# Moving the load of w1 behind GpSimd's filter copies and its half of V's reorder

## The chip, the cores and the metric

The kernel runs on one core of one Trainium2 chip. The core has five engines that matter here: TensorE (PE, matmuls; PEld is its weight load), VectorE (DVE), ScalarE (ACT), GpSimd (POOL) and SyncE (SP), and 16 DMA engines that all queues share. The metric is the device time of one execution in microseconds (us), lower is better. Before the change it is 516.92 us, the median of 3 runs (514.62 to 517.74).

## The reference

Two blocks follow each other on x of 8 batches x 3136 rows x 256 columns. The first is a global filter: a Fourier transform along the 3136 rows, a product with a complex filter, and the inverse transform. The second mixes rows by a product of rank 32 (U, V) and then columns by two matrices with a ReLU between them:

```python
X = np.fft.rfft(x, axis=1)
Y = X * (filt_r + 1j * filt_i)[None]
x = np.fft.irfft(Y, n=3136, axis=1)            # output of the first block
h = x.transpose(0, 2, 1) @ U @ V               # rank 32
u = x + h.transpose(0, 2, 1)
out = u + np.maximum(u @ w_ch1, 0) @ w_ch2     # w_ch1 256x1024, w_ch2 1024x256
```

## The kernel before, in words

All arrays are float16, the output is float32. The transform of 3136 = 49 x 64 points is done in steps by matmul against constant matrices, one batch at a time:

- f1: over the 49, from the loaded x (tile `x`, four loads of 392 KB a batch, L128). For batches 0 and 1 its result is turned on TensorE (`turn`), for the others it goes through HBM.
- mid: over the 64 (pz, L384), the product with the filter (DVE `uv`, L392) and the inverse over the 64 (pe, L345). ScalarE copies the result into tiles `e` (L355), two frequencies k at a time. For each batch 12 such pairs are made; I call them pair 0 to pair 11. From `e`, SP writes them to HBM (`ct`, L364), two pairs in one DMA of 256 KB, and reads them back in another order into the tile `eb` (`load_e2`, L416), because the next step needs k along the partitions. Batch 0 differs: pairs 8, 9 and pair 10 are written by two DMAs (256 KB and 128 KB), and pair 11 goes straight from `e` into `eb` by four DMAs of 32 KB, two issued by GpSimd and two by SP (L359). The read back into `eb` of batch 0 comes in six DMAs: three for its first half (h=0) and three for its second (h=1).
- rank (ph, L423): the product with U, copied 64 times into `eb` by DVE (L438).
- s4 (pu, L456): the inverse over the 49 and the product with V together, 16 groups of 8 matmuls, from `eb` and the tile `sv`. `sv` holds the constants and V in another order of its columns; that reorder is done half by GpSimd and half by DVE (`v_rows`, L201). The first eight groups read the first half of `eb`, the other eight the second half.
- Then the two matrices, over 49 groups of 512 rows: mm1 (phh, L488) with `w1sb`, ReLU on ScalarE (L491), mm2 (pc, L544) with `w2sb`, and the residual (L536).

The schedule is written out by hand: each engine runs its instructions in the order in which the program emits them, and waits in front of one that isn't ready. Batch 0 runs alone as a prologue (lines 581 to 625); after that the plan (lines 564 to 659) deals the steps of the next batches between the matmuls of mm1 and mm2.

DMAs go through two queues. q0 holds what GpSimd issues: the loads of U, x, the filters (`fab`, three parts), V (`vnat`), the constants of `sv`, w1 and w2, and the stores of the output. q1 holds what SP issues: `ct` and `eb`. Within each queue, on each of the 16 DMA engines, the DMAs stand in order of issue. On SP, a read back into `eb` that waits for its `ct` writes also holds up the `ct` writes that the program emits behind it. SP's order in the prologue is: write pairs 0-1, 2-3, 4-5, 6-7; read back part 0 of h=0 (it waits for the writes of pairs 0-1 and 2-3); write pairs 8-9; write pair 10; read back part 1 of h=0; two rows of pair 11; read back part 2 of h=0 (it waits for the writes of pairs 8-9 and 10); then the three parts of h=1.

The second copy of the filter (partitions 64 to 127) is made by copies on the chip, `spread_filters` (L167): parts 0 and 1 by DVE and ScalarE, part 2 by GpSimd in four copies. Later on GpSimd wait the copies `seen` (L620): each reads a few elements of `eb`, and so holds GpSimd until a half of `eb` has landed; behind them come the other loads of x of batch 1 and the load of w2 (L623).

Of the kernel before, what the change touches and what calls it, by code (L numbers as in the profile page):

```python
# [80 lines left out]
def kernel(  # L81
# [11 lines left out]
    nc = tc.nc  # L93
# [31 lines left out]
    def load_x(b, c):  # L125
        t = sb.tile([98, 8 * DM], F16, tag="x", bufs=4, name="x")
        for a, n in ((0, 96), (96, 2)) if b == 0 else ((0, 98),):
            nc.gpsimd.dma_start(t[a:a + n], dram(x.tensor, (b * SEQ + 8 * c + 32 * a) * DM, [[32 * DM, n], [1, 8 * DM]]))  # L128
        xt[b, c] = t
# [30 lines left out]
    def spread_filters(i):  # L160
        s = slice(PARTS[i], PARTS[i + 1])
        copies = ((nc.vector.tensor_copy, nc.scalar.copy), (nc.vector.tensor_copy, nc.scalar.copy),
                  (nc.gpsimd.tensor_copy, nc.gpsimd.tensor_copy))[i]

        for s in (slice(PARTS[2], 19), slice(19, NK)) if i == 2 else (s,):
            for f, copy in enumerate(copies):
                copy(fab[64:128, f, s, :], fab[0:64, f, s, :])  # L167
# [12 lines left out]
    w1sb = cst.tile([128, 2, NH], F16)  # L180
# [19 lines left out]
    def v_rows(copy, a, z):  # L200
        copy(sv[0:RANK, a:z], vnat.rearrange("p (q r) -> p r q", r=NR)[:, a:z])  # L201
# [34 lines left out]
    def u_copied(pt):  # L236
        nc.scalar.copy(uh[:, 1:, :].rearrange("r k u -> r (k u)"), pt[:, RANK:RANK * (NK + 2)])
        nc.scalar.copy(uh[0:NR, 0, :], pt[0:NR, 0:RANK])
# [173 lines left out]
    def load_e2(b, part, hs=(0, 1)):  # L412

        n = 12 if (b, part) == (0, 2) else 16
        for h in hs:
            nc.sync.dma_start(eb[32 + part:32 + 4 * n:4, 32 * h:32 * h + 32, :].rearrange("p (q r) d -> p q (r d)", r=8),  # L416
                              dram(ct2[b][part], 8 * h * DM, [[NR * DM, n], [16 * DM, 4], [1, 8 * DM]]))
# [172 lines left out]
        next(f1s[0])  # L590
    nc.gpsimd.dma_start(sv[32:97], sv_d.rearrange("k (r q) -> k r q", q=NQ))
    load_x(1, 0)
    nc.gpsimd.dma_start(w1sb, moe_w_ch1.rearrange("(h dd) c -> dd h c", h=2))
    spread_filters(2)
    v_rows(nc.gpsimd.tensor_copy, 0, 32)
    for i in range(13):
        next(mids[0])
        if i == 8:
            u_copied(put)
        if i == 10:  # L600
            load_e2(0, 0, [0])
# [88 lines left out]
```

## Time and profile before

| | us |
|---|---|
| median of 3 runs | 516.92 |
| the profiled execution, its own time | 516.43 |
| its span | 514.6 |
| PE busy, over the span | 490.5 (95%) |
| DVE busy | 366.2 (71%) |
| ACT busy | 377.1 (73%) |
| POOL busy | 80.6 (16%) |
| issue of w1 on GpSimd | 21.07, took 0.76, landed 13.3 after its start |
| first weight load from w1 (L488) | 49.7 |
| issue of w2 on GpSimd | 48.87, landed 10.5 after its start |
| granted TensorE clock, mean | 0.995 of full |

The page gives the span's busy time of each engine, the costliest groups of instructions, and the chain of work that ended last. A position such as 35.61 is in us from the start of the span. The time of a DMA "to landing" runs from the start of its issue to the event that its waiters see. Answers on a stretch of the trace tell what was busy in it, and per DMA queue the packets, the megabytes (MB) and the time that these packets took as a share of 16 engines' time in the stretch; the shares of both queues may add up to over 100%.

### The profile page before, as it was taken

To read this page: it belongs to the slowest core of one execution; us is meant where nothing else is said; L and a number is where in the kernel's file an instruction comes from. 1 tells how busy PE (TensorE), PEld (TensorE's weight loads), DVE (VectorE), ACT (ScalarE), POOL (GpSimd) and SP (SyncE) were. 2 spreads that over 40 slices of the span, in tenths; PEclk is the share of its full clock that TensorE was granted. 3 is DMA by queue.
4 is the path that set the end of the run, shared out by engine and by line. 5 is a ranking of instruction groups with operands and counts; after the bars stand their busy time and mean duration, and the time that the engine had idled before them with its cause. 6 is when DMAs were issued, how large, how long until landed. Compare 5 with 4: busy or idle time off the path is not lost.

```text
span 514.6 us, 11909 instructions
## 1 busy us (share of the span) xinstructions
PE 490.5 (95%) x4754; PEld 349.6 (68%) x4754; DVE 366.2 (71%) x497; ACT 377.1 (73%) x704; POOL 80.6 (16%) x122
## 2 busy tenths in 40 slices
PE   3887899999999999999999999999999998999996
PEld 3645566776767777777767777777677765676665
DVE  5886599579847986679747986679846997853332
ACT  6874778867986689667986689667886676666663
POOL 6662010002001110002001110002001000011110
PEclk9998999999999999999999999999999999999999
DMA  8987926957877286837877286837877136644454
GB/s 187 175 206 174 181 74 172 281 171 176 216 229 251 69 186 190 298 130 177 213 227 254 69 185 202 262 156 184 218 228 240 65 126 206 212 153 149 126 162 163
DMA packets 76016, 94.52 MB, mean 184 GB/s; under 512 B 5795, under 2 KB 58979, under 8 KB 75960
## 3 DMA queue, kind: packets, MB, share of 16 engines
q1 hardware_dynamic: 61256, 52.17, 33.9%
q0 software_dynamic: 14704, 41.58, 31.4%
q8 instruction: 37, 0.61, 0.5%
q14 instruction: 19, 0.16, 0.1%
HBM read 58.35 MB, written 50.92 MB: 212 GB/s over the span
## 4 chain that ended last, share of the span: by engine, by line
PE 81%; DVE 8%; DMA 4%; issue 1%; ACT 1%; SPq 0%; POOL 0%; DVEq 0%; POOLq 0%
PE pc L544 31%; PE phh L488 30%; DVE uv L392 5%; PE pu L456 5%; PE pf L250 4%; PE pe L345 4%; PE pz L384 3%; PE pc L536 3%; DMA w2sb<-in_moe_w_ch_dram 2%; PE ph L423 1%; DVE uv L397 1%; DMA eb<-ct 1%; DVE uv L396 1%; DMA ct<-e 1%; DVE och L556 1%
## 5 line engine op out<-in xcount | busy, mean ns | idle before, releaser
L491 ACT ACTIVATE h<-phh 128x512 f16<-128x512 f32 x392 | 235.9, 603 | 83.2 <-PE phh L488 81.7
L544 PE MATMUL pc<-w2sb,h 128*128 128x256 f16 x1568 | 233.7, 272 | 1.2 <-DMA w2sb<-in_moe_w_ch_dram 1.2
L488 PE MATMUL phh<-ut,w1sb 128*128 128x512 f16 (+7 forms) x896 | 233.3, 352 | 0.4 <-DVE ut L463 0.4
L544 PEld LDWEIGHTS <-h 128*128 128x128 f16 x1568 | 151.7, 97 | 91.8 <-issue 1.5
L392 DVE TENSOR_TENSOR uv<-pz,fab 128x1024 f16<-128x1024 f32 (+1 forms) x104 | 120.6, 1177 | 12.5 <-PE pz L384 10.5
L561 POOL DMA_DIRECT2D out_dram<-och x48 | 39.1, 814 | 402.0 <-DVE och L556 318.8
L488 PEld LDWEIGHTS <-w1sb 128*128 128x128 f16 x896 | 78.9, 97 | 19.8 <-issue 1.5
L556 DVE COPY och<-pc 128x512 f32<-128x512 f32 x74 | 51.0, 689 | 44.4 <-PE pc L536 43.5
L355 ACT CAST e<-pe 128x512 f16<-128x512 f32 x96 | 56.6, 591 | 21.0 <-PE pe L345 20.2
L463 DVE CAST ut<-pu 128x392 f16<-128x392 f32 x92 | 48.5, 557 | 17.9 <-PE pu L456 16.0
L255 ACT CAST asb<-pf 98x512 f16<-98x512 f32 x96 | 57.3, 599 | 0.2
L438 DVE COPY eb<-h 32x4096 f16<-32x4096 f16 x32 | 38.2, 1232 | 14.2 <-ACT h L435 14.2
L552 DVE TENSOR_TENSOR och<-pc,tur 128x512 f32<-128x512 f32 x24 | 16.5, 689 | 39.8 <-PE pc L544 37.3
L345 PE MATMUL pe<-uv,m 128*128 128x512 f16 (+1 forms) x117 | 41.3, 371 | 3.6 <-DVE uv L392 1.5
L456 PE MATMUL pu<-sv,eb 97*128 97x49 f16 x1024 | 40.5, 187 | 3.3 <-DMA eb<-ct 3.1
L456 PEld LDWEIGHTS <-eb 97*128 97x128 f16 x1024 | 37.7, 98 | 4.8 <-DVE eb L438 3.4
L536 PE MATMUL pc<-idn,ut 128*128 128x128 f16 (+1 forms) x302 | 40.8, 219 | 0.0
L384 PE MATMUL pz<-a,m 128*128 128x512 f16 x96 | 36.2, 379 | 1.1 <-DVE a L311 1.0
L250 PE MATMUL pf<-x,ws 98*98 98x256 f16 x192 | 36.6, 273 | 0.0
L396 DVE TENSOR_TENSOR uv<-uv 64x1024 f16<-64x1024 f16 (+1 forms) x49 | 30.9, 630 | 1.7
L536 PEld LDWEIGHTS <-ut 128*128 128x128 f16 (+1 forms) x302 | 28.8, 98 | 3.9 <-issue 0.6
L397 DVE TENSOR_TENSOR uv<-uv 64x1024 f16<-64x1024 f16 (+1 forms) x49 | 30.7, 627 | 0.7
(80 smaller groups left out, 264.9 us busy)
## 6 DMA issues: line engine op xcount, KB each, us to landing
out_dram<-och POOLq DMA_DIRECT2D x48, 512.0 KB, 4.4
ct<-e SPq DMA_DIRECT2D x47, 256.0 KB
eb<-ct SPq DMA_DIRECT2D x46, 256.0 KB
x<-in_x_dram POOLq DMA_DIRECT2D x28, 392.0 KB, 7.8
ct<-asb SPq DMA_DIRECT2D x24, 384.0 KB
a<-ct SPq DMA_DIRECT2D x18, 512.0 KB
tu<-tu SPq DMA_DIRECT2D x48, 64.0 KB
tur<-tu SPq DMA_DIRECT2D x12, 256.0 KB
```

Of the source, the lines that this page charges most:

```text
L250: nc.tensor.matmul(pf[0:98, 256 * s:256 * s + 256], ws[:, (8 * c + j) * 98:(8 * c + j + 1) * 98], t[:, j, :], start=(s == 0), stop=True, s ...
L255: nc.scalar.copy(dst, src)
L345: nc.tensor.matmul(pe[:, 0:n], w, uv[:, f, o:o + n], start=(f == 0), stop=(b > 0 or f == 1))
L355: nc.scalar.copy(t[:, 2 * (i % 2):2 * (i % 2) + 2, :].rearrange("p k d -> p (k d)"), pe)
L384: nc.tensor.matmul(pz, a2m, src[:, k:k + 2, :].rearrange("p k d -> p (k d)"), start=True, stop=True)
L392: nc.vector.tensor_mul(uv[:, :, o:o + n], zin, fin)
L456: nc.tensor.matmul(pu[:, NQ * i:NQ * i + NQ], eb[:, 8 * n + i, d], sv[:, 8 * g + i, :], start=(i == 0), stop=True, skip_group_check=True)
L488: nc.tensor.matmul(ph[:, o:o + n], w1sb[:, dh, 128 * t:128 * t + 128], utv(b)[:, dh, t0:t0 + n], start=(dh == 0), stop=(dh == 1), skip_gro ...
L491: nc.scalar.activation(h, ph, RELU)
L536: nc.tensor.matmul(d, w, idn, start=False, stop=(dh == 1), skip_group_check=True)
L544: nc.tensor.matmul(o, gr.h[tt][:, 128 * i:128 * i + 128], w2sb[:, tt, :], start=(tt == 0), stop=(tt == 7 and turned(gr)), skip_group_check ...
L556: nc.vector.tensor_copy(gr.och[:, i - 1:i + 1, :], gr.pc.rearrange("p (j d) -> p j d", d=DM))
```

## The change

The issue of the load of w1 (512 KB, one DMA of GpSimd's queue) moves from in front of GpSimd's four filter copies and its copy of V to behind them. On GpSimd it then stands in front of the two row DMAs of pair 11 (L359). No other engine's order of instructions changes, and nothing is added or removed.

```diff
     nc.gpsimd.dma_start(sv[32:97], sv_d.rearrange("k (r q) -> k r q", q=NQ))
     load_x(1, 0)
-    nc.gpsimd.dma_start(w1sb, moe_w_ch1.rearrange("(h dd) c -> dd h c", h=2))
     spread_filters(2)
     v_rows(nc.gpsimd.tensor_copy, 0, 32)
+    nc.gpsimd.dma_start(w1sb, moe_w_ch1.rearrange("(h dd) c -> dd h c", h=2))
     for i in range(13):
         next(mids[0])
```

## Prediction

> **What bounds the kernel now.** The page's first part has PE busy for 95% of the span, and the chain that ended last is 81% PE. So a microsecond lost or won in the prologue (batch 0, before the matmuls of mm1 and mm2 fill PE) is carried to the end: in the main part nothing is idle to take it up. I therefore read the chain in order of time up to 62 us:
>
> ```profile
> 36.57 0.37 ACT e L355
> 36.94 3.57 DMA ct<-e
> ...
> 42.77 4.31 DMA eb<-ct
> ...
> 47.28 0.19 POOL seen L620
> ...
> 48.87 10.53 DMA w2sb<-in_moe_w_ch_dram
> 59.41 0.04 issue
> 59.45 0.60 PE pc L544 x4
> ```
>
> Columns: start, length, what. The last `ct` write of batch 0 (pair 10) goes out at 36.94 and lands at 40.5; then SP issues the last four read-backs into `eb`, the last of which lands at 47.1; only then `seen` lets GpSimd issue the rest of x and w2, and the first mm2 waits for w2 until 59.45. From the landing of pair 10's write on the distances are fixed: 40.5 to 47.1 to 59.45. **The landing of pair 10's write is the clock of the prologue.** w1 is not in this chain.
>
> Next, GpSimd's timeline, to see where w1 stands and where it will stand:
>
> ```profile
> 21.07 0.76 POOL L593 DMA_DIRECT2D w1sb<-in_moe_w_ch_dram x1
> 24.18 1.46 POOL L167 COPY fab<-fab 64x1536 f16<-64x1536 f16 x1 [2.35 <-DMA fab<-in_filt_r_dram]
> 26.53 4.28 POOL L167 COPY fab<-fab 64x1536 f16<-64x1536 f16 x3 [0.89 <-DMA fab<-in_filt_i_dram]
> 30.87 2.90 POOL L201 COPY sv<-vnat 32x1568 f16<-32x1568 f16 x1
> 37.45 1.08 POOL L359 DMA_DIRECT2D eb<-e  x2 [3.68 <-ACT e L355]
> ```
>
> The brackets give idle time before the line and what ended it. The copies wait for filter data, not for the issue of w1, and after the last copy (33.77) GpSimd is idle for 3.68 us.
>
> Third, SP's timeline, for the writes and read-backs:
>
> ```profile
> 27.87 5.02 SPq L364 DMA_DIRECT2D ct<-e  x3
> 35.61 0.59 SPq L416 DMA_DIRECT2D eb<-ct  x1
> 36.31 1.07 SPq L364 DMA_DIRECT2D ct<-e  x2
> 37.47 0.53 SPq L416 DMA_DIRECT2D eb<-ct  x1
> ```
>
> The first read-back (35.61) waited from 32.9 on, 2.6 us in all, for the writes of pairs 0-1 and 2-3, issued at 25.61 and 27.87: SP's semaphore events stand at 34.7 and 35.5, so they took 9.1 and 7.6 us. Behind it the writes of pairs 8-9 and 10 were late: their data was ready at 34.61 and 35.75 (ACT's copies of 0.59 us from 34.02 and 35.16), they went at 36.31 and 36.94.
>
> Why did the writes take so long? The DMA queues from 29 to 30 us, and from 33 to 34 us (packets, MB, share of 16 engines):
>
> ```profile
> q0 software_dynamic: 74, 0.16, 82.1%
> q1 hardware_dynamic: 120, 0.06, 23.6%
> ```
>
> ```profile
> q1 hardware_dynamic: 590, 0.29, 97.6%
> q0 software_dynamic: 6, 0.01, 5.4%
> ```
>
> While GpSimd's q0 has bytes, SP's q1 gets 0.06 to 0.09 MB a us (28 to 32 us; none at all before 28); when q0 is dry it gets 0.29. From 28 us on q0 moves 0.66 MB, of which w1 is 0.52; x(1,0), in front of it, landed at 20.52 + 9.8 = 30.3, w1 at 34.4. So **w1 is what starves the `ct` writes from about 28.7 to 33.3 us.** Then, from 35 to 37 us, both queues stand nearly still (0.08 and 0.02 MB).
>
> **The change, part by part.**
>
> 1. *GpSimd's own time.* 0.76 us leaves 21.07 and comes back at 33.77. Cost and gain 0: the copies wait until 24.18 and 26.53 for filter DMAs which stand in q0 ahead of w1 in both kernels (issues 17.53 + 6.5 and 18.62 + 7.8), and the 0.76 us lie in the idle 3.68. Without that cover it would be 0.76 on the rows of pair 11. w1's own wait is for an earlier filter DMA on its semaphore, landed long before. Behind w1 on GpSimd wait only the two row DMAs (37.45), which wait for ACT anyway.
>
> 2. *The early `ct` writes lose their competitor.* Pairs 0-1, 2-3 and one row DMA are 0.55 MB. From 28.7 at 0.29 MB/us they take 1.9 us; with x's tail until 30.3 I say 31.0. In the trace the event came 2.1 us behind the byte count (0.55 MB were reached at 33.4, the event at 35.5): 33.1. SP is free at 32.89, so the first read-back goes at 33.2 instead of 35.61. Behind it pairs 8-9 go at 34.65 and pair 10 at 35.8, when ACT is done: **pair 10 is issued 1.1 us earlier** (35.8 against 36.94). More can't be won there.
>
> 3. *The late writes get w1 as their competitor.* w1 is issued at 33.77; q0's first packets show some 1.2 us after an issue (x at 44.86, packets from 46 on), so it flows from 35.0, at first alone (0.24 MB/us, 25 to 27 us): 0.25 MB by 36.05, when the packets of pairs 8-9 come (1.4 us after their issue, as with the read-back of 35.61). The other 0.27 MB goes at 0.16 MB/us, the row above: until 37.75. q1 moves some 0.12 MB of its 0.39 meanwhile (pairs 8-9 and 10), the other 0.27 at 0.29: 38.7. In the trace pair 10's event stood 1.0 us behind its bytes: landing at 39.7 against 40.55. **Sum: 0.85 us earlier.**
>
>    This is an estimate from rows of another stage, so both ends are kept. If w1 held up nothing, 0.39 MB from 36.05 would be through at 37.4 and landed by 38.5: 2.0 us won. If pair 10 were held up as long as pairs 2-3 were (7.6 us), it would land at 43.4: 2.9 us lost. I take the value between, because w1 is half through, in an otherwise idle stretch, before the last writes compete.
>
> 4. *The rows of pair 11* stand behind w1 in q0; they landed at about 42, are first read at 44.28, and w1's last bytes are through by about 38. Cost 0. If w1 ran on to 44 they would decide, 1 for 1.
>
> 5. *w1's own user.* The first weight load from it is at 49.7. Even at its old 13.3 us, w1 lands at 47.1. Cost 0, 2.6 us of cover.
>
> 6. *What is late next.* s4 waits for the first half of `eb` (PE idle 3.10 us until 44.28), but DVE's copies of rank into `eb` (L438) end at 43.29 in both. The first half can give 0.9 at most, the second half, which carries w2's chain, the whole 0.85.
>
> The Trainium skill has a rule that speaks against the new place (SBUF — State Buffer, section SBUF: two separate sides): a DMA issued by GpSimd needs GpSimd to write its descriptors, and a two-port DVE copy locks it out meanwhile. DVE's fast copies (L438, 1.21 us each) run from 38.67 to 43.29; from 33.77 to 38.67 DVE runs the filter products and a slower copy. By the rule w1 would suffer only if its descriptors took over 4.9 us; the sum by it is the same 0.85, and at the worst w1 lands after 43.29. No run here shows that yet.
>
> Sum: 516.43 (the profiled execution, 514.6 of span and 1.8 around it) less 0.85 is **515.6 us**. The median of the three runs lies 0.5 above the profiled execution and their spread is 3.1, so the effect is smaller than that spread.
>
> **The rivals.**
>
> *A, slower: w1 starves the last writes.* Mechanism: the same queue sharing, now at 35 to 40 us on the chain's own write. For it: the 9.1 and 7.6 us above. Against it: w1 is alone in q0, without the 0.4 MB of x and more ahead of it. It decides once pair 10 takes over 4.7 us from its issue at 35.8 (then it lands after 40.5). Price at 7.6 us: +2.9, 519.3; at 9.1: +4.4, 520.8.
>
> *B, nothing happens:* the gain of step 2 and the loss of step 3 cancel (pair 10 takes 4.7 us). 516.4.
>
> *C, the clock.* After the 3.10 us wait s4 runs at a falling clock; the windows (PE, PEld, DVE, ACT, POOL, clock, DMA share, GB/s) show it:
>
> ```profile
> 44.00:45.00 1.00, 0.72 (x26) 0.75 (x27) 0.00 (x0) 0.01 (x1) 0.50 (x3) 1.00 0.78 250
> 45.00:46.00 1.00, 1.00 (x30) 1.00 (x27) 0.85 (x2) 0.95 (x2) 0.44 (x1) 0.61 0.46 168
> 46.00:47.00 1.00, 1.00 (x26) 1.00 (x24) 0.82 (x3) 0.50 (x2) 0.00 (x0) 0.50 0.70 119
> ```
>
> A group takes 0.43 us there instead of 0.265. If a wait of 2.3 us no longer costs the clock, s4's first half ends ahead of the second half's landing (46.35), its second half takes 8 x 0.265 = 2.1 us and ends at 48.5 instead of 49.05: 0.55 more, 515.0. Against it: w2's chain, untouched by the clock, still ends last. The Trainium skill (TensorE: Matmul & The Clock Gate, Part 1: The HAM clock gate) has the clock halve after an idle window of some 3.4 us; the trace shows the half after a gap of 3.10, so the rule doesn't say where 2.3 falls.
>
> *D, w1 late for mm1:* w1 would have to take over 15.9 us; each us more costs 1. At 18 us, 518.5.
>
> **How the numbers follow.** Forecast (515.6, give or take 1): 0.45. B: 0.18. A: 0.2. C: 0.14. D: 0.03. Within 1% is 511.8 to 522.1, about what a measurement of this kernel can tell from no change; all the cases priced lie inside. I leave 0.04 for slower than that (A with D) and 0.02 for faster. Range: down to the 2.0 of step 3 (514.4) with the runs' spread below it, up to A at 7.6 us: 513.8 to 519.3.
>
> **What would show it.** In the profile after: w1 issued at 33.8 and landed before 42; the first read-back on SP near 33.2, the `ct` writes of pairs 8-9 and 10 at 34.7 and 35.8; q1 near 0.29 MB/us from 31 us on, and q0 busy from 35 to 38; pair 10 landing near 39.7, the first s4 matmul near 43.4, `seen` near 46.4, the first mm2 near 58.6. I am wrong if the early writes still land after 34.6 (then not w1 but something else starves them), or if pair 10 lands after 40.5 (then A).

## Result, and the profile after

| | before | after |
|---|---|---|
| median, us (22 runs each, side by side) | 515.56 (513.48 to 518.97) | 517.38 (516.32 to 519.78) |
| ratio | 1 | 1.0034, 95% interval 1.0019 to 1.0049 |
| profiled execution: its time, its span | 516.43, 514.6 | 519.31, 517.5 |

The change makes the kernel 0.34% slower, 1.8 us. That is small, but the interval leaves out 1. I had forecast 0.85 us faster. The profiled execution after lies 1.9 us above its own median, so sizes read from it are on the high side; I take the sign from it and the size from the medians.

The same three views as before. The chain up to the first mm2 (start, length, what):

```profile
35.14 0.60 ACT e L355
35.73 0.02 issue
35.75 6.30 DMA ct<-e
...
44.31 4.47 DMA eb<-ct
...
48.99 0.19 POOL seen L620
...
50.59 11.65 DMA w2sb<-in_moe_w_ch_dram
62.24 0.04 issue
62.28 0.60 PE pc L544 x4
```

It is the chain of before, link by link, with one link of another length: the write of pair 10 starts 1.2 us earlier (35.75 against 36.94) and takes 6.30 us in place of 3.57. It lands at 42.05, against 40.5. SP's timeline:

```profile
33.10 0.59 SPq L416 DMA_DIRECT2D eb<-ct  x1
34.62 1.49 SPq L364 DMA_DIRECT2D ct<-e  x2
36.20 0.57 SPq L416 DMA_DIRECT2D eb<-ct  x1
37.16 1.15 SPq L359 DMA_DIRECT2D eb<-e  x2
42.11 2.99 SPq L416 DMA_DIRECT2D eb<-ct  x4
```

The first read-back went from 35.61 to 33.10 and the writes of pairs 8-9 and 10 follow at 34.62 and 35.75: the early half of the plan works. Then SP stands until 42.11. GpSimd's timeline has w1 at its new place:

```profile
31.55 2.89 POOL L201 COPY sv<-vnat 32x1568 f16<-32x1568 f16 x1
34.39 0.74 POOL L595 DMA_DIRECT2D w1sb<-in_moe_w_ch_dram  x1
37.43 1.09 POOL L359 DMA_DIRECT2D eb<-e  x2 [2.29 <-ACT e L355]
```

And the two queues, from 36 to 37 us and from 38 to 39 us (packets, MB, share of 16 engines):

```profile
q0 software_dynamic: 17, 0.03, 55.7%
q1 hardware_dynamic: 47, 0.02, 8.5%
```

```profile
q0 software_dynamic: 81, 0.17, 92.8%
q1 hardware_dynamic: 76, 0.04, 18.9%
```

w1 (q0) has hardly started when the writes of pairs 8-9 and 10 (q1) want to go, and from 37 to 40 us it takes four fifths of the bytes. Behind the first mm2 nothing differs in these two profiles: from there to the end of the span it is 455.1 us before (514.6 less 59.45) and 455.2 after. The whole difference between them is in the prologue. Over all the profiles below that stretch takes 455.0 to 456.9 us, so a single execution can also lose a microsecond or two behind the prologue.

### The profile page after: what moved, and what is told of

Same layout as the page of the kernel before. It is cut to its first block, busy times and chain, and to the rows that moved or that the text cites. A ratio compares the mean times of both kernels' runs of the same rounds, so it can differ in the third digit from the quotient of the medians.

```text
span 517.5 us, 11909 instructions
## 1 busy us (share of the span) xinstructions
PE 491.2 (95%) x4754; PEld 349.8 (68%) x4754; DVE 366.6 (71%) x497; ACT 376.8 (73%) x704; POOL 80.9 (16%) x122
## 4 chain that ended last, share of the span: by engine, by line
PE 77%; DVE 8%; DMA 6%; ACT 1%; issue 1%; SPq 0%; POOL 0%; DVEq 0%; POOLq 0%; ACTq 0%
PE pc L544 29%; PE phh L488 28%; DVE uv L392 5%; PE pu L456 5%; PE pf L250 4%; PE pe L345 3%; PE pz L384 3%; PE pc L536 3%; DMA ct<-e 2%; DMA w2sb<-in_moe_w_ch_dram 2%; DMA eb<-ct 2%; DVE uv L397 1%; PE ph L423 1%; DVE uv L396 1%; DVE och L556 1%
## 5 line engine op out<-in xcount | busy, mean ns | idle before, releaser
L392 DVE TENSOR_TENSOR uv<-pz,fab 128x1024 f16<-128x1024 f32 (+1 forms) x104 | 120.8, 1179 | 12.6 <-PE pz L384 10.4
L438 DVE COPY eb<-h 32x4096 f16<-32x4096 f16 x32 | 38.2, 1232 | 14.2 <-ACT h L435 14.2
L456 PE MATMUL pu<-sv,eb 97*128 97x49 f16 x1024 | 41.6, 189 | 4.7 <-DMA eb<-ct 4.6
L456 PEld LDWEIGHTS <-eb 97*128 97x128 f16 x1024 | 38.9, 99 | 6.4 <-issue 5.2
```

Source lines behind the costliest of these rows:

```text
L392: nc.vector.tensor_mul(uv[:, :, o:o + n], zin, fin)
L456: nc.tensor.matmul(pu[:, NQ * i:NQ * i + NQ], eb[:, 8 * n + i, d], sv[:, 8 * g + i, :], start=(i == 0), stop=True, skip_group_check=True)
```

## Experiments

Theory: w1 holds up whichever of SP's writes it travels beside, at the old place the early `ct` writes of batch 0, at the new place the last ones; each place has its price in us, and the new one's is higher. Rivals: the loss comes from the clock (PE was idle 4.62 us ahead of s4, and all of s4 ran at half clock); from GpSimd's descriptors being late; or from bytes alone, wherever they stand.

Since executions start up to 0.8 us apart, I count from the end of DVE's twelve filter products (L392), a mark that none of the edits is aimed at. "Pair 10 out" is the start of its issue on SP. "Landed" is when SP goes on to the last four read-backs: the writes of pairs 8-9 and 10 have both landed by then, and SP's rows of pair 11, which stand ahead, are issued. Those five columns come from one profiled execution of each kernel, the last two from all its runs. The ratios are those of each set against the kernel before in the same set (its median over the sets is 515.70), with 12 runs of each variant (9 of the one with an eighth of w1, 22 of the first row "after").

| kernel | first read-back | pair 10 out | landed | first s4 | first mm2 | median us | ratio (95%) |
|---|---|---|---|---|---|---|---|
| before | 0.00 | 1.33 | 4.96 | 8.67 | 23.84 | 515.7 | 1 |
| after | -2.49 | 0.16 | 6.52 | 10.19 | 26.69 | 517.38 | 1.0034 (1.0019 to 1.0049) |
| after, again | -2.54 | 0.16 | 5.72 | 9.23 | 25.60 | 517.46 | 1.0024 (1.0002 to 1.0047) |
| an eighth of w1 | -2.53 | 0.16 | 2.87 | 6.52 | 21.28 | 514.17 | 0.9970 (0.9956 to 0.9983) |
| w1 at both places | -0.30 | 1.03 | 6.06 | 9.43 | 24.66 | 516.83 | 1.0025 (1.0005 to 1.0045) |
| w1 behind pair 11's rows | -2.23 | 0.17 | 2.81 | 6.70 | 25.21 | 517.3 | 1.0032 (1.0008 to 1.0056) |
| after, w1 in 512 B pieces | -2.53 | 0.17 | 6.61 | 10.22 | 25.79 | 517.95 | 1.0033 (1.0017 to 1.0049) |
| after, V's DVE half later | -2.53 | 0.16 | 5.59 | 9.41 | 23.01 | 517.19 | 1.0027 (1.0006 to 1.0048) |
| after, PE kept busy | -2.53 | 0.17 | 6.84 | 10.21 | 24.27 | 517.31 | 1.0025 (1.0005 to 1.0045) |
| half and half | -1.31 | 0.17 | 3.43 | 7.86 | 23.27 | 514.91 | 0.9987 (0.9965 to 1.0009) |
| w1 ahead of V's reorder | -2.54 | 0.16 | 4.66 | 8.04 | 22.19 | 515.24 | 0.9985 (0.9966 to 1.0004) |
| the same, again | -2.54 | 0.15 | 3.93 | 8.02 | 22.70 | 515.40 | 0.9980 (0.9956 to 1.0004) |
| half old place, half ahead of V's reorder | -1.48 | 0.16 | 3.35 | 6.90 | 23.36 | 515.15 | 0.9971 (0.9941 to 1.0001) |
| four quarters | -1.71 | 0.16 | 4.55 | 7.92 | 23.45 | 515.26 | 0.9982 (0.9958 to 1.0005) |

The first mm2 also carries what the loads of x and w2 behind it took in that one execution (w2 alone 9.0 to 11.7 us), so it scatters by 1 to 2 us; the columns left of it are steadier.

### The two places priced: an eighth of w1, and w1 twice

```diff
-    nc.gpsimd.dma_start(w1sb, moe_w_ch1.rearrange("(h dd) c -> dd h c", h=2))
+    nc.gpsimd.dma_start(w1sb[:, :, 0:128], moe_w_ch1.rearrange("(h dd) c -> dd h c", h=2)[:, :, 0:128])
...
-w1sb[:, dh, 128 * t:128 * t + 128]
+w1sb[:, dh, 0:128]
```

> The changed kernel with an eighth of w1 loaded (64 KB in place of 512 KB, at the place behind the copies) and that eighth used for all eight column blocks of mm1: seven eighths of w1 are left out, the instructions of all engines stay the same in number and shape. So neither place carries w1's bytes. Competition theory (w1 at the old place delays the early ct writes, at the new place the last ones, and from there both go 1 for 1 to the end): pair 10 is issued as in the changed kernel (0.1 us after the end of DVE's filter products) and lands within 3.2 us of its issue; the first mm2 comes 1.5 to 2.5 us earlier than before; time 0.996 to 0.9975 of before. Rival (w1's bytes are hidden at the old place, and the loss has another cause than bytes, the place of the issue itself): time as before or as the changed kernel, 1.000 to 1.003.

Measured: 514.17 us, 0.997 (0.9956 to 0.9983), as the competition theory had it. Pair 10's write in the chain of this kernel, and the end of SP's timeline:

```profile
35.12 2.65 DMA ct<-e
```

```profile
36.53 1.15 SPq L359 DMA_DIRECT2D eb<-e  x2
37.83 3.02 SPq L416 DMA_DIRECT2D eb<-ct  x4
```

SP's instructions up to the rows of pair 11 are those of the changed kernel, less the 0.6 us by which this execution started earlier; the last read-backs come 1.3 us behind the start of these rows in place of 5. The instructions are the same, at the same places, and w1 still goes in 256 packets, now of 256 B, so it is w1's bytes that hold up pair 10, not the place of the issue. The two places now have prices, from the medians: the old one 515.7 less 514.17, **1.5 us**; the new one 517.44 (all runs of the changed kernel) less 514.17, **3.3 us**. The change is the difference.

The second load, for the other corner:

```diff
+    w1d = sb.tile([128, 2, NH], F16, tag="och", bufs=2, name="w1d")
+    nc.gpsimd.dma_start(w1d, moe_w_ch1.rearrange("(h dd) c -> dd h c", h=2))
     spread_filters(2)
     v_rows(nc.gpsimd.tensor_copy, 0, 32)
     nc.gpsimd.dma_start(w1sb, moe_w_ch1.rearrange("(h dd) c -> dd h c", h=2))
```

> w1 is loaded twice: at the old place into a tile that nobody reads (512 KB more), and at the new place into its own. Competition theory: the early writes are as late as before (pair 10 issued about 1.2 us after the end of DVE's products) and the last ones as slow as in the changed kernel (5 to 6.5 us to landing, a little less as w1 is half through by then); pair 10 lands 1.5 to 2.5 us later than before the change; time 1.004 to 1.006 of before, that is over the changed kernel by what the old place costs. Rival (one load is hidden by the other, only the later one counts): as the changed kernel, 1.003.

Measured: 516.83 us, 1.0025 (1.0005 to 1.0045). The prices don't add up: their sum over the kernel with an eighth of w1 would be 4.8 us, measured are 2.7, no more than the new place alone. The rival was right on the time. The table shows how: the early load does delay the first read-back and pair 10 again (out at 1.03), but w1's second load is under way by then, and pair 10 lands no later (6.06) than in the changed kernel (5.72 and 6.52). From 36 to 37 us of this kernel q0 has the engines for itself; q1 has no packet at all, though the write of pairs 8-9 was issued at 35.19:

```profile
q0 software_dynamic: 90, 0.18, 112.7%
```

### Is it the clock?

```diff
-    for i in range(10):
+    for i in range(30):
         if i < 4:
             next(f1s[1])
         unread(pw, 1)
```

> The changed kernel with 20 more matmuls of 128x512 whose result nobody reads, ahead of s4, so that PE is busy from 40.9 to about 45.3 us instead of idle for 4.6 us. They change no value that is used. Clock theory: the clock stays at 1.00 through s4, its groups follow at 0.265 us in place of 0.435 where nothing else holds them, s4 ends at about 51 in place of 52.5, limited by the second half of eb (48.9), and x and w2 are used earlier; the first mm2 comes at 61.5 or earlier in place of 62.28; time 0.15% to 0.4% under the changed kernel. Rival (w2's chain decides, the clock is beside it): s4 is faster but the first mm2 stays at 62.0 to 62.3, and the time is 1.003 of before.

Measured: 517.31 us, 1.0025 (1.0005 to 1.0045). The groups of s4 now follow at 0.26 us and the window from 45 to 46 us has a granted clock of 1.00 (PE, PEld, DVE, ACT, POOL, clock, DMA share, GB/s):

```profile
45.00:46.00 1.00, 0.82 (x29) 0.85 (x29) 0.00 (x0) 0.11 (x1) 0.60 (x3) 1.00 0.85 242
```

mm1 starts 2.1 us earlier than in the first profile of the changed kernel (15.30 against 17.41 in the table's count), though not earlier than in the second (15.22), where the write landed 1.1 us sooner than here. The first mm2 came earlier than in both (24.27 against 26.69 and 25.60), which the clock theory had expected; but w2's load alone took 9.81 us here and 11.65 and 11.68 there, so a single profile doesn't decide this. The time decides: it doesn't move beyond its interval. So the half clock is not what made the changed kernel slower; it follows from the wait for `eb`, and in these profiles w2, which hangs on the same `eb`, comes last. That isn't always so: with V's DVE half later, the chain up to the first mm2 runs through s4 at half clock and not through w2. A gain of some tenths can't be excluded.

### Is it GpSimd's descriptors, or the size of w1's packets?

In the first profile w1 started slowly while DVE's half of V's reorder ran (35.50 to 36.98), so I moved that copy behind DVE's copies of rank:

```diff
-    v_rows(nc.vector.tensor_copy, 32, NR)
     next(ranks[0])
     for _ in ranks[0]:
         pass
+    v_rows(nc.vector.tensor_copy, 32, NR)
```

> The changed kernel, with DVE's half of V's reorder moved behind its copies of rank into eb, so that DVE runs nothing from 35.5 to 38.7 us. Descriptor theory (DVE's SBUF to SBUF copy keeps GpSimd from writing w1's descriptors; q0 moved only 0.03 MB from 36 to 37 us and 0.15 from 37, when that copy ends at 36.98): q0 moves at least 0.10 MB from 36 to 37 us, w1 lands at about 40.2 in place of 41.1, pair 10 at 41.2 in place of 42.05. Rival (any load of GpSimd's needs some 2.5 us to come up to speed, whatever DVE does): q0 moves 0.03 MB from 36 to 37 us, and pair 10 lands at 42.0. Time by the first 0.1% to 0.2% under the changed kernel, by the second the same (1.003 of before).

Measured: 517.19 us, 1.0027 (1.0006 to 1.0048). q0 moved 0.06 MB from 36 to 37 us, between the two expectations, but w1 was issued at 31.88 here, 2.5 us earlier than in the first profile, so this is not the same stage. The profile to compare with is the second one of the changed kernel, with the issue at 32.22: from 34 to 37 us q0 moved 0.08, 0.07 and 0.06 MB a us without the copy, and 0.05, 0.08 and 0.07 with it. w1 landed 7.4 us after its issue in both (6.7 in the first profile), and pair 10 landed at 5.59 against 5.72. So the copy is not the cause. What stays of the rival is the slow start itself: in the profiles with all of w1 at or near the new place, 2.5 to 5 us pass from its issue until it moves 0.13 MB a us or more, with the copy and without. Its cause stays open.

The other try at the mechanism cut w1 into pieces of 512 B:

```diff
-    w1sb = cst.tile([128, 2, NH], F16)
+    w1sb = cst.tile([128, 4, 2, 256], F16)
...
-    nc.gpsimd.dma_start(w1sb, moe_w_ch1.rearrange("(h dd) c -> dd h c", h=2))
+    nc.gpsimd.dma_start(w1sb, moe_w_ch1.rearrange("(h dd) (s c) -> dd s h c", h=2, c=256))
```

> The changed kernel, with w1 in pieces of 512 B in place of 2 KB (another order of columns in its tile, read accordingly by mm1; same bytes, same place of issue). Turn-taking theory: while w1 flows, SP's queue moves as many bytes as w1, 0.09 to 0.12 MB a us in place of 0.04; pair 10 lands at 40.5 to 41.2 in place of 42.05, the first s4 matmul at 44.2 to 45.0, w1 itself later (42 to 44); time 0.1% to 0.3% under the changed kernel, that is 1.000 to 1.002 of before. Rival, bytes alone: pair 10 lands at 42.0 as in the changed kernel, or later because small packets are slower, and the time is 1.003 of before or more.

Measured: 517.95 us, 1.0033 (1.0017 to 1.0049), pair 10 landed at 6.61. From 36 to 37 us the queues answer with one line:

```profile
q0 software_dynamic: 280, 0.14, 126.4%
```

w1's packets are a quarter as large and about four times as many as the 73 to 81 a us of the changed kernel, and q1 has none in this us, nor in the next (0 against 303). Its writes were due: with an eighth of w1, where SP's writes are issued within 0.2 us of these, q1 moves 512 and 148 packets in the same two us. That the queues take turns packet by packet would have given q1 its half. The turn-taking theory falls as an account of these us, though it fits others (81 packets against 76 from 38 to 39 us of the changed kernel). Turns of many packets at a time are not excluded, and by what rule the engines choose between the queues stays open; what the runs show is that a load of GpSimd's that is under way can go through almost alone for two us.

### Later: behind the rows of pair 11

```diff
-    nc.gpsimd.dma_start(w1sb, moe_w_ch1.rearrange("(h dd) c -> dd h c", h=2))
     for i in range(13):
...
     next(ranks[0])
     next(mids[0])
+    nc.gpsimd.dma_start(w1sb, moe_w_ch1.rearrange("(h dd) c -> dd h c", h=2))
     v_rows(nc.vector.tensor_copy, 32, NR)
```

> w1 is issued behind the two row DMAs of pair 11 on GpSimd (about 38.5 us), so neither the early nor the last ct writes of batch 0 have it beside them. Turn-taking theory (each DMA engine takes one packet of each queue in turn, so a 2 KB packet of w1 costs each 512 B packet of a ct write four times its own time): pair 10, issued at 35.8, lands at about 38.5 to 39.0 (3 us or less after its issue, against 6.3 with w1 in front of the rows and 3.6 before the change); the first s4 matmul comes at 43.4 to 43.8, the first mm2 at 58 to 59; time 0.2% to 0.4% under before. Rival, bytes alone (the same 0.52 MB must be moved before w2 somewhere in the prologue, wherever it stands): the last read-back of eb lands at 47 or later as w1 is then beside the read-backs; time as before, within 0.1%.

Measured: 517.3 us, 1.0032 (1.0008 to 1.0056). SP is as early at the last read-backs as with an eighth of w1 (2.81), s4 starts at 6.70, and all of it is lost again on the last read-back, in the chain of this kernel:

```profile
37.98 0.88 SPq L416
...
40.46 8.39 DMA eb<-ct
...
48.94 0.49 PE pu L456 x8
```

8.39 us in place of the 4.31 before the change. From 42 to 43 us w1 shares the engines with the read-backs, and both are slow:

```profile
q0 software_dynamic: 59, 0.12, 66.6%
q1 hardware_dynamic: 30, 0.07, 22.2%
```

I was right on pair 10 and wrong on the end: the bytes have only met the next link of the same chain. The rival had the last read-back right (48.85, said 47 or later), but not the time, which it had as before the change.

### Earlier or in parts

The whole of w1 in front of GpSimd's half of V's reorder, run twice, and then three ways of splitting it over several places. First the whole:

```diff
     spread_filters(2)
+    nc.gpsimd.dma_start(w1sb, moe_w_ch1.rearrange("(h dd) c -> dd h c", h=2))
     v_rows(nc.gpsimd.tensor_copy, 0, 32)
-    nc.gpsimd.dma_start(w1sb, moe_w_ch1.rearrange("(h dd) c -> dd h c", h=2))
```

> w1 is issued between GpSimd's filter copies and its half of V's reorder, some 2.9 us earlier than in the changed kernel. Competition theory: w1 starts to flow at about 31 to 32.5 us, when the writes of pairs 0 to 3 are through, and is through before pairs 8-9 and 10 go out or soon after; pair 10 is issued 0.1 to 0.6 us after DVE's products and lands in 3 to 4.5 us; time 0.998 to 1.000 of before, the best place. Rival (whatever is issued behind the copies meets the last writes, as GpSimd's loads flow for 5 us or more): 5.5 us or more to landing and 1.002 to 1.003 of before.

> The kernel with w1 between the filter copies and GpSimd's half of V's reorder once more, for a narrower interval. Competition theory: 0.998 to 0.9995 of before, pair 10 at 4 to 5 us from issue to landing. Rival (the first reading was noise, the place gives nothing): 1.000, give or take 0.001.

Measured: 515.24 and 515.40 us, 0.9985 (0.9966 to 1.0004) and 0.9980 (0.9956 to 1.0004). The landings are as the competition theory had them: 4.66 and 3.93 are ahead of the 4.96 before; the times alone don't tell it from the rival of the second run. w1 is issued 4.5 and 5.7 us ahead of the end of DVE's products (1.2 and 2.8 in the two profiles of the changed kernel), and its packets are through about when pair 10's begin. From 33 to 35 us q1 has next to nothing (0 and 8 packets a us in the second profile). By SP's order what stood there were above all the writes of pairs 6-7; that they can spare the time is argued, not shown.

```diff
+    nc.gpsimd.dma_start(w1sb[:, 0, :], moe_w_ch1[0:128, :])
     spread_filters(2)
     v_rows(nc.gpsimd.tensor_copy, 0, 32)
-    nc.gpsimd.dma_start(w1sb, moe_w_ch1.rearrange("(h dd) c -> dd h c", h=2))
+    nc.gpsimd.dma_start(w1sb[:, 1, :], moe_w_ch1[128:256, :])
```

> One half of w1 (256 KB, its first 128 rows) at the old place and the other half at the new one. Competition theory in proportion to bytes: pair 10 issued 0.1 to 0.8 us after the end of DVE's products, landing 4.2 to 5.2 us after its issue; time 1.001 to 1.002 of before. Rival (any load that is in flight when pair 10 goes out costs the same, because it is the start of the load that hurts): 6 us to landing and 1.003 of before or more.

Measured: 514.91 us, 0.9987 (0.9965 to 1.0009), better than expected: pair 10 is out at 0.17 and lands at 3.43. Half of w1 behind V's reorder does not cost half of 3.3 us but, within the noise, next to nothing: its 256 KB are through by 36 us, and from 36 to 37 us q1 has the engines (418 packets against none of q0). The rival (the start of a load is what hurts) falls.

With the second half moved one place forward:

```diff
     spread_filters(2)
+    nc.gpsimd.dma_start(w1sb[:, 1, :], moe_w_ch1[128:256, :])
     v_rows(nc.gpsimd.tensor_copy, 0, 32)
-    nc.gpsimd.dma_start(w1sb[:, 1, :], moe_w_ch1[128:256, :])
```

> One half of w1 at the old place, the other between the filter copies and GpSimd's half of V's reorder. If the cost of a place grows faster than its bytes (half of w1 behind V's reorder cost some 0.1 us, the whole 3.3): the second half costs next to nothing, the first half of what the whole does at the old place, 0.8 us; time 0.9980 to 0.9990 of before. If cost goes with bytes at either place: 0.9985 to 0.9995, as the two whole placements.

Measured: 515.15 us, 0.9971 (0.9941 to 1.0001), landed at 3.35; the interval holds both expectations. And in four quarters, the second issued between GpSimd's second and third filter copy:

```diff
+    nc.gpsimd.dma_start(w1sb[:, 0, 0:512], moe_w_ch1[0:128, 0:512])
     spread_filters(2)            # w1sb[:, 0, 512:1024] is issued behind its first two copies
+    nc.gpsimd.dma_start(w1sb[:, 1, 0:512], moe_w_ch1[128:256, 0:512])
     v_rows(nc.gpsimd.tensor_copy, 0, 32)
-    nc.gpsimd.dma_start(w1sb, moe_w_ch1.rearrange("(h dd) c -> dd h c", h=2))
+    nc.gpsimd.dma_start(w1sb[:, 1, 512:1024], moe_w_ch1[128:256, 512:1024])
```

> w1 in four DMAs of 128 KB: at the old place, behind GpSimd's first two filter copies, behind the last two, and behind its half of V's reorder. If cost grows faster than bytes, spreading is best: 0.9970 to 0.9985 of before, near the kernel without w1's bytes (0.997). If cost goes with bytes: 0.9985 to 1.000. Each further DMA costs GpSimd about 0.55 us of issue, which delays its copies by 1.1 us at most, in front of nothing that waits.

Measured: 515.26 us, 0.9982 (0.9958 to 1.0005), landed at 4.55. The readings of these placements (0.9971 to 0.9987) can't be told apart, nor any one from the kernel before: each interval includes 1, though all five medians lie 0.4 to 0.8 us under that of the kernel before in their set. Whether cost grows faster than bytes is so not decided by the times. Against the changed kernel they are 2 us faster (515.24 and 515.40 against 517.38 and 517.46).

The changed kernel again, measured beside the last three:

> The changed kernel once more, beside the three below, and for a second profile. If w1 is in front of the last ct writes whenever it is issued ahead of them: pair 10 takes 5 to 7 us to landing here too, and while w1 flows SP's queue moves less than a quarter of what GpSimd's moves. If the 6.3 us of the first profile were chance: 3.5 to 4.5. Time 1.002 to 1.005 of before. DVE's half of V's reorder runs as before; if it holds up w1's start, q0 is below 0.05 MB in the us in which it ends.

Measured: 517.46 us, 1.0024 (1.0002 to 1.0047); pair 10 took 5.50 us. q0 moved 0.07 MB from 36 to 37 us, so the 0.03 of the first profile is not the rule, but the long write is. q1's share is not below a quarter throughout here: it was 0.11 MB against 0.07 in that us, the 4 KB packets of a read-back; the 512 B packets of the writes came behind.

## Why the prediction was wrong, point by point

- **What bounds the kernel: right.** The chain after has the same links; pair 10's landing, the read-backs, `seen`, w2 and the first mm2 follow each other as said, and the 455 us behind it are unchanged in the first pair of profiles.
- **Step 1, GpSimd's own time: right.** 0.74 us at the new place, in idle time.
- **Step 2, the early writes: right in size.** First read-back 33.10 (said 33.2), pairs 8-9 34.62 (34.65), pair 10 35.75 (35.8). The kernel with an eighth of w1 shows what the old place cost: 1.5 us.
- **Step 3, the late writes: this step failed.** It had pair 10 land 3.9 us after its issue; it took 6.30 and 5.50. The mechanism, two queues on the same engines, was right; the terms for w1 were mis-sized, all to the good side. First, the flow: I had w1 start 1.2 us after its issue at full rate, half through by 36.05 and through by 37.75, 4.0 us after its issue. In the first profile it was issued at 34.39, because the filters landed 0.6 us later, had moved 0.04 MB by 37.0 and was through at about 40, 5.6 us after its issue. The late issue isn't the reason: in the second profile w1 was issued at 32.22 and its last bytes came at about 39, 6.8 us after. Second, the rate "at first alone (0.24 MB/us)". Of the two us it was read from, the second is:

```profile
q0 software_dynamic: 69, 0.24, 99.9%
```

  These packets have 3.5 KB on average; w1 then stood behind other loads in q0. w1 goes in packets of 2 KB, and with the engines for itself it moved at most 0.18 to 0.20 MB a us (w1 twice, PE kept busy, w1 ahead of V's reorder). Third, q1's share: I let it move some 0.07 MB a us beside w1, by the rows from 29 us on. I passed over the us before, from 28 to 29 us, with q0 still full:

```profile
q0 software_dynamic: 63, 0.19, 96.4%
q1 hardware_dynamic: 37, 0.02, 6.2%
```

  So "0.06 to 0.09 MB a us (28 to 32 us)" was a misreading; from 28 to 32 us q1 gets 0.02, 0.06, 0.07 and 0.09 while q0's share falls from 96% to 59%. Beside w1 at its new place the `ct` writes got 0.04 (37 to 40 us, q0 at 85 to 93%), and nothing at all for a us or two in three other profiles (w1 twice, w1 in small pieces, PE kept busy). In the first profile the range's upper end, pair 10 as slow as pairs 2-3, was nearer than the value between.
- **Steps 4 and 5, pair 11's rows and w1's own user: right.** w1 landed at 41.1; mm1 did not wait for it.
- **Step 6: the bound was wrong, without effect here.** The first half of `eb` didn't come earlier, so DVE's end at 43.29 didn't matter. Where it did come earlier, s4 started ahead of that end (41.48 with an eighth of w1, DVE's copies ending at 42.65): s4's first eight groups read only the half of `eb` that the first two of DVE's four copies fill.
- **The rule on descriptors**, weighed and not counted: no run shows that DVE's V copy delays w1. DVE's fast copies do hold up GpSimd, see below.
- **The rivals.** A was the one that happened, at less than its price: +1.5 us on pair 10's landing in the first profile, +0.8 in the second, and +1.8 in the median, against +2.9. I gave it 0.2. C had the wrong sign: the wait grew to 4.62 us, the clock was at half through all of s4, and keeping it at full won nothing beyond the interval.

## What to carry to other kernels

A load that is "not needed yet" has a price where it flows, not where it is issued: list what the other queue must move in the 2 to 8 us behind the issue, and whether one of those transfers is a link of the chain. Here 512 KB cost 1.5 us beside writes with some slack, 3.3 beside the last writes and about as much (517.3 less 514.17) beside the read-backs, while half of it fitted into the gap for next to nothing. So try to split a load, or to move it by one instruction, before moving it past everything; here that undid the loss, but no such placement was shown to beat the kernel before. Weigh a load by the time that its packets take on the engines, not by its bytes alone: w1 moved 0.18 MB in a us at 112.7% of the engines' time (w1 twice), the `ct` writes 0.29 MB at 97.6% (before, 33 to 34 us). And take the share that a queue gets under competition from a stretch in which both queues are full, not from one in which one of them runs dry.

## What the runs showed of the hardware that I had not expected

- While a load of w1 was under way, SP's queue of 512 B writes could get no packet for a us or more, whether w1 went in packets of 2 KB (0 against 90 from 36 to 37 us with w1 twice) or of 512 B (0 against 280 and 303 from 36 to 38 us). In other stretches the two queues moved about equal numbers of packets (76 against 81).
- A load of GpSimd's came up to speed slowly: w1, issued at 32.48 in the kernel with PE kept busy, moved 0.03 MB from 35 to 36 us, 0.10 in the next and 0.19 in the third.
- GpSimd is held up by DVE's float16 copies (L438). With w1 behind the rows of pair 11 those copies ran from 38.24 to 42.89, and what fell beside them on GpSimd took longer: the issue of w1 1.49 in place of 0.74 us, the first pair of `seen` copies 1.39 in place of 0.42 us:

```profile
38.12 1.49 POOL L605 DMA_DIRECT2D w1sb<-in_moe_w_ch_dram  x1
41.79 1.39 POOL L620 COPY seen<-eb 32x4 f16<-32x4 f16 x2 [2.18 <-DMA eb<-ct]
...
49.06 0.41 POOL L620 COPY seen<-eb 32x4 f16<-32x4 f16 x2 [5.36 <-DMA eb<-ct]
```

  With an eighth of w1 the pair took 1.31 us beside these copies, too. This fits what the Trainium skill says (SBUF — State Buffer, section SBUF: two separate sides): a DVE copy in a two-port mode and GpSimd share a port pair, and the one that comes second waits. The trace doesn't show in which mode these copies run.
- The clock halved after a wait of 3.10 us (before) and stayed at 1.00 after one of 2.46 us (w1 ahead of V's reorder), but it halved after one of 2.44 us (the same, again: 0.54 from 45 to 46 us) and after one of 2.27 us (half and half, where it is at 0.50 from 43 to 46 us), so the length of one wait does not decide it here.
